# K blocks transposed by DMA instead of by TensorE, in a two-layer decode kernel

## The chip, the cores and the metric

One core of one Trainium2 chip (trn2). The metric is device time of one execution in microseconds (us), on the core. Before the change it is 217.3 us (median of 2 runs, 216.55 to 218.04). A profile's span is 1.7 to 1.9 us shorter than the time of the same run.

## The reference

Decode for a batch of 4, one new token each. Two rounds of attention over a cached window and a gated feed-forward layer (GLU), with the same K, V and weights in both rounds:

```python
x = x + A(layernorm(x), k_cache, v_cache, wq, wo)
x = x + B(layernorm(x), w_gate, w_up, w_down)
x = x + A(...)      # the same caches and weights again
x = x + B(...)

def A(x, k_cache, v_cache, wq, wo):            # B=4, Hq=32, Hkv=8, Dh=128
    W = 2048                                   # last 2048 of 8192 keys
    q = (x @ wq)                               # 4 query heads share one K/V head
    p = softmax(q @ k[:, :, -W:, :].T * Dh**-0.5)
    return (p @ v[:, :, -W:, :]) @ wo
```

There are 32 K blocks and 32 V blocks (8 heads, 4 sequences), each 2048 x 128 bf16, 512 KB.

## The kernel before

The first attention layer loads each K block in a staging slot of SBUF, transposes it on TensorE, and copies it from PSUM to its resident place in `kt`. The second attention layer finds K there and reads V alone again. A list scheduler in the program orders the instructions of each engine; all DMAs are issued by SyncE, in program order.

```python
def kv_d(cache, b, h):          # partition p gets keys 16p..16p+15: rows of 4 KB
    return cache[b, h, SK - W:SK, :].rearrange("(p j) d -> p (j d)", p=128)

def k_head(h):                  # the four K blocks of one head
    for b in range(NB):
        i = h * NB + b
        s = load_block(...)                     # one of 9 staging slots ("arena")
        for t in range(NHALF):                  # 2 halves of 8 columns of 128x128
            # TensorE: 8 transposes into one PSUM bank
            #   pe.transpose(bankb(bank)[:, jj*128:(jj+1)*128], src[:, j*128:(j+1)*128], ident_b)
            # VectorE or ScalarE in turn: copy 128x1024 to kt[:, i*SLOT + ...]
            ...  # cut
        pool.release(s, rel_names)

def e_s(pe, ...):               # scores: K^T is the stationary operand
    for j in range(NJ):         # 16 slices of 128 keys
        pe.matmul(ps[...], kt[:, i*SLOT + j*128 : i*SLOT + (j+1)*128], qT[...])

# program order in the first layer, which is the order of the DMA queue:
#   K(0), wq, then for each head h:  K(h+1), scores(h), V(h), wo(h), PV(h), output(h)
# V, wq and the GLU weights use the same 9 slots.        ... the rest is cut
```

Of the kernel before, what the change touches and what calls it, by code (L numbers as in the profile page):

```python
# [244 lines left out]
class _SlotPool:  # L245
# [29 lines left out]
    bw_4k=338.0, bw_1k=292.0, bw_8k=350.0,  # L275
# [6 lines left out]
def build(nc, A_x, A_k, A_v, A_wq, A_wo, B_wg, B_wu, B_wd, out, cfg=None):  # L282
    cfg = dict(cfg or {})
    tm = dict(_TM)
# [7 lines left out]
    _, HKV, SK, DH = A_k.shape  # L292
    HQ = A_wq.shape[1] // DH
    REP = HQ // HKV
    W = min(4096, max(256, SK // 4))
    NJ = W // 128
# [5 lines left out]
    SLOT = NJ * 128  # L302
# [4 lines left out]
    TB = min(8, NJ)  # L307
    NHALF = NJ // TB
# [20 lines left out]
    def kv_d(cache, b, h):  # L329
        return cache[b, h, SK - W:SK, :].rearrange("(p j) d -> p (j d)", p=128)  # L330

    es = contextlib.ExitStack()
    with es:
        def sb(name, shape, dt):
            return es.enter_context(nc.sbuf_tensor(name, shape, dt))

        kt = sb("kt", [128, NBLK * SLOT], BF16)
        wo_sb = sb("wo_sb", [128, HKV * WOH], BF16)
        arena = sb("arena", [128, NA * SLOT], BF16)
        ident_b = sb("ident_b", [128, 128], BF16)  # L340
# [32 lines left out]
        for _pass in range(cfg.get("passes", 1)):  # L373
            P = _Plan()
            pool = _SlotPool(range(NA), slot_est)

            def slot_ap(s):
                if s < NA:
                    return arena[:, s * SLOT:(s + 1) * SLOT]
                i = s - NA  # L380
                return kt[:, i * SLOT:(i + 1) * SLOT]

            def slot_tok(s):
                if s < NA:
                    return (("slot", s),)
                i = s - NA
                return tuple(("kt", i, t) for t in range(NHALF))
# [4 lines left out]
            def bankb(b):  # L392
                return ps[:, b, :].bitcast(BF16)

            def c_dve(n, rate=None):
                return tm["dve_fix"] + n * (tm["dve_f32"] if rate is None else rate)

            def c_act(n):
                return tm["act_fix"] + n * tm["act_el"]

            def c_pairs(n):
                return n * tm["pe_pair"]

            def dma(name, dst, src, w, r=(), rate="bw_4k", nbytes=None, sem=None):
                if nbytes is None:
                    nbytes = dst.partition_size() * dst.free_nbytes()
                o = P.op("sync", name, 0.0, lambda e, dst=dst, src=src: e.dma_start(dst, src),
                         r=r, w=w, dma_bytes=nbytes, dma_rate=tm[rate])
                if sem is not None:
                    o.sem = sem  # L410
                    o.inc = 16
                return o
# [5 lines left out]
                 r=[("ones_f",)], w=[("ident_f",)])  # L418
            P.op("gpsimd", "ident_b", 200.0, lambda g: g.tensor_copy(ident_b[:], ident_f[:]),
                 r=[("ident_f",)], w=[("ident_b",)])  # L420
# [4 lines left out]
            def emit_xT_in(t):  # L425
                last = None
                for c in range(NC):
# [4 lines left out]
                 w=[("psx", QB)], banks=(QB,))  # L432
            P.op("vector", "xT_cp", c_dve(NX), lambda v: v.tensor_copy(xT[:, :], bankb(QB)[:, 0:NX]),
                 r=[("psx", QB)], w=[("xT",)], banks=(QB,))
# [39 lines left out]
            def load_block(name, cache, b, h):  # L474
                s = pool.alloc()
                dma(name, slot_ap(s), kv_d(cache, b, h), w=slot_tok(s))
                return s

            def attention(L, first, banks):
                TBK = banks["T"]  # L480
# [4 lines left out]
                tcount = [0]  # L485

                def k_head(h):
                    for b in range(NB):
                        i = h * NB + b
                        s = load_block("K%d_%d_%d" % (L, h, b), A_k, b, h)  # L490
                        rel_names = []
                        for t in range(NHALF):
                            bank, ev = TBK[tcount[0] % len(TBK)]
                            tcount[0] += 1

                            def e_tr(pe, s=s, t=t, bank=bank):
                                last = None
                                src = slot_ap(s)
                                for jj in range(TB):
                                    j = t * TB + jj  # L500
                                    last = pe.transpose(bankb(bank)[:, jj * 128:(jj + 1) * 128],  # L501
                                                        src[:, j * 128:(j + 1) * 128], ident_b[:, :])
                                return last
                            P.op("tensor", "T%d_%d_%d" % (L, i, t), TB * tm["pe_tr"], e_tr,
                                 r=list(slot_tok(s)) + [("ident_b",)], w=[("pst", bank)], banks=(bank,))
                            rel_names.append("T%d_%d_%d" % (L, i, t))
                            dst = kt[:, i * SLOT + t * TB * 128: i * SLOT + (t + 1) * TB * 128]
                            if ev == "vector":
                                P.op("vector", "evT%d_%d_%d" % (L, i, t), c_dve(TB * 128, tm["dve_bf_psum"]),
                                     lambda v, dst=dst, bank=bank: v.tensor_copy(dst, bankb(bank)[:, 0:TB * 128]),  # L510
                                     r=[("pst", bank)], w=[("kt", i, t)], banks=(bank,))
                            else:
                                P.op("scalar", "evT%d_%d_%d" % (L, i, t), c_act(TB * 128),
                                     lambda a, dst=dst, bank=bank: a.copy(dst, bankb(bank)[:, 0:TB * 128]),  # L514
                                     r=[("pst", bank)], w=[("kt", i, t)], banks=(bank,))
                        pool.release(s, rel_names)

                if first:
                    k_head(0)
                first_q = True  # L520
                for ktc in range(NC):
                    for qc in range(NQCH):
                        s = pool.alloc()
# [5 lines left out]
                        def e_q(pe, ktc=ktc, q0=q0, q1=q1, s=s, st=first_q):  # L529
                            last = None  # L530
                            src = slot_ap(s)
                            for q in range(q0, q1):
# [8 lines left out]
                             r=list(slot_tok(s)) + [("xn",)], w=[("psq", QB)], banks=(QB,))  # L541
# [4 lines left out]
                     r=[("psq", QB)], w=[("qT",)], banks=(QB,))  # L546

                def scores_softmax(h):
# [5 lines left out]
                    for b in range(NB):  # L554
                        i = h * NB + b

                        def e_s(pe, i=i, b=b, h=h, sbk=sbk):
                            last = None
                            for j in range(NJ):
                                c0 = b * NJ * REP + j * REP  # L560
                                last = pe.matmul(ps[:, sbk, c0:c0 + REP],  # L561
                                                 kt[:, i * SLOT + j * 128: i * SLOT + (j + 1) * 128],
                                                 qT[:, b * HQ + h * REP: b * HQ + (h + 1) * REP],
                                                 start=True, stop=True)
                            return last
                        P.op("tensor", "S%d_%d" % (L, i), c_pairs(NJ), e_s,
                             r=[("kt", i, t) for t in range(NHALF)] + [("qT",)],
                             w=[("pss", sbk, b)], banks=(sbk,))
# [4 lines left out]
                         r=[("pss", sbk, b) for b in range(NB)], w=[("m1", kd)], banks=(sbk,))  # L573
                    P.op("tensor", "smaxT_%d_%d" % (L, h), tm["pe_small"],
                         lambda pe, m1v=m1v, mbk=mbk: pe.transpose(ps[0:NR, mbk, 0:128], m1v, ident_f[:, :]),  # L575
                         r=[("m1", kd), ("ident_f",)], w=[("psm", mbk, 0)], banks=(mbk,))
# [3 lines left out]
                         r=[("psm", mbk, 0)], w=[("gmv", kd)], banks=(mbk,))  # L580
# [3 lines left out]
                         r=[("gmv", kd), ("ones_f",)], w=[("Gb", kd)])  # L584
                    P.op("tensor", "smaxB_%d_%d" % (L, h), tm["pe_small"],
                         lambda pe, Gv=Gv, mbk=mbk: pe.transpose(ps[:, mbk, 128:128 + NR], Gv, ident_f[0:NR, 0:NR]),  # L586
                         r=[("Gb", kd), ("ident_f",)], w=[("psm", mbk, 1)], banks=(mbk,))
# [3 lines left out]
                         r=[("psm", mbk, 1)], w=[("gbc", kd)], banks=(mbk,))  # L591
# [7 lines left out]
                         r=[("pss", sbk, b) for b in range(NB)] + [("gbc", kd)], w=[("d", kd)], banks=(sbk,))  # L599
                    ev = ebuf[:, ke * GC:(ke + 1) * GC]  # L600
                    P.op("scalar", "sexp_%d_%d" % (L, h), c_act(GC),
                         lambda a, ev=ev, dv=dv: a.activation(ev, dv, ACTF.Exp, scale=SCALE),  # L602
                         r=[("d", kd)], w=[("e", ke)])
                    esv = esum[:, kd * NR:(kd + 1) * NR]
                    P.op("vector", "ssum_%d_%d" % (L, h), c_dve(GC),
                         lambda v, ev=ev, esv=esv: v.tensor_reduce(  # L606
                             esv.rearrange("p (b r) -> p b r", b=NB),
                             ev.rearrange("p (b j r) -> p b r j", b=NB, j=NJ, r=REP), AXX, ALU.add),
                         r=[("e", ke)], w=[("es", kd)])
# [3 lines left out]
                         r=[("es", kd), ("ones_f",)], w=[("psm", mbk, 2)], banks=(mbk,))  # L613
# [3 lines left out]
                         r=[("psm", mbk, 2)], w=[("rinv", ke)], banks=(mbk,))  # L617
# [59 lines left out]
            def glu(L, banks):  # L677
# [49 lines left out]
                for (fc0, fc1) in bounds:  # L727
# [24 lines left out]
                T=[(0, "vector"), (2, "scalar"), (1, "vector"), (3, "scalar")], S=[4], M=[6], O=5)))  # L752
# [5 lines left out]
                 r=[("xT",)], w=[("xb16",)])  # L758

            def e_out_tr(pe):  # L760
                last = None
                for c in range(NC):
# [3 lines left out]
                 w=[("pso_f", QB)], banks=(QB,))  # L766
            P.op("vector", "out_cp", c_dve(D, tm["dve_bf_psum"]), lambda v: v.tensor_copy(o_nat[:, :], bankb(QB)[0:NB, 0:D]),
                 r=[("pso_f", QB)], w=[("xnat",)], banks=(QB,))
# [77 lines left out]
```

## Time and profile before

The span splits at the layer norms. This is the timeline of TensorE, at the first matmul of the norm before each layer; columns are start (us), duration (us), engine, line and instruction.

```profile
121.16 0.59 PE L438 MATMUL ps<-lr,ones_f 128*128 128x4 f32 x2 [0.48 <-DVE lr L440]
...
133.00 0.59 PE L438 MATMUL ps<-lr,ones_f 128*128 128x4 f32 x2 [0.48 <-DVE lr L440]
...
202.63 0.59 PE L438 MATMUL ps<-lr,ones_f 128*128 128x4 f32 x2 [0.48 <-DVE lr L440]
```

| stage | ends at | length, us |
|---|---|---|
| first attention layer | 121.16 | 121.2 |
| first GLU | 133.00 | 11.8 |
| second attention layer | 202.63 | 69.6 |
| second GLU, output | 215.5 | 12.9 |

The table of windows has a row for each stretch: its length, then the busy time and instruction count of each engine, the granted TensorE clock, the busy share of the 16 DMA engines (the times of the packets are added up, so it passes 1.0 where they overlap: up to 23 are under way at once in this trace), and GB/s.

```profile
36.00:74.00 38.00, 32.23 (x631) 30.89 (x630) 16.15 (x37) 13.62 (x18) 0.00 (x0) 0.72 1.03 398
74.00:111.00 37.00, 31.23 (x647) 30.03 (x645) 14.62 (x35) 13.62 (x18) 0.00 (x0) 0.68 1.01 373
111.00:121.00 10.00, 4.44 (x114) 3.78 (x111) 2.67 (x10) 0.59 (x2) 0.00 (x0) 0.50 0.79 291
121.00:133.00 12.00, 6.64 (x172) 6.04 (x172) 2.07 (x10) 0.60 (x3) 0.00 (x0) 0.50 0.98 311
144.00:170.00 26.00, 18.65 (x545) 17.70 (x546) 7.95 (x27) 1.77 (x6) 0.00 (x0) 0.50 1.03 408
```

In the first attention layer both sides are nearly full: the DMA engines have a share of 1.0 at about 400 GB/s, and TensorE is busy 85% of the time. The DMA engines are ahead by a hair; from 74 us on the rate sags to 373 GB/s, and from 111 to 121 us there is a hole while TensorE finishes the last head.

The groups of instructions that the change touches (busy time in us, mean ns of one, then the engine's idle time before them), and the K transfers (count, KB each, median us from issue to landing):

```profile
L501 PE MATMUL ps<-ident_b,arena 128*128 128x128 bf16 x512 | 47.5, 279 | 1.1 <-DMA arena<-in_A_k_cache_dram 1.1
...
L514 ACT COPY kt<-ps 128x1024 bf16<-128x1024 bf16 x32 | 31.5, 1015 | 49.9 <-PE ps L501 49.9
L561 PEld LDWEIGHTS ps<-qT,kt 128*128 128x128 bf16 x1024 | 30.6, 102 | 15.9 <-issue 7.8
...
L510 DVE COPY kt<-ps 128x1024 bf16<-128x1024 bf16 x32 | 22.1, 692 | 27.1 <-PE ps L501 27.1
```
```profile
arena<-in_A_k_cache_dram SPq DMA_DIRECT2D x32, 512.0 KB, 8.9
```

So 47.5 us of TensorE work and 53.6 us of copies are to go. The mean of 279 ns is a duration with overlap: 512 x 279 ns would be 143 us. And this is how a burst of score matmuls looks in the timeline: 16 in 0.55 us, about 34 ns each.

```profile
69.52 0.55 PE L561 MATMUL ps<-qT,kt 128*128 128x4 bf16 x16 [0.72 <-DVE dbuf L594]
```

### The profile page before, as it was taken

To read this page: it belongs to the slowest core of one execution; us is meant where nothing else is said; L and a number is where in the kernel's file an instruction comes from. 1 tells how busy PE (TensorE), PEld (TensorE's weight loads), DVE (VectorE), ACT (ScalarE), POOL (GpSimd) and SP (SyncE) were. 2 spreads that over 40 slices of the span, in tenths; PEclk is the share of its full clock that TensorE was granted. 3 is DMA by queue.
4 is the path that set the end of the run, shared out by engine and by line. 5 is a ranking of instruction groups with operands and counts; after the bars stand their busy time and mean duration, and the time that the engine had idled before them with its cause. 6 is when DMAs were issued, how large, how long until landed. Compare 5 with 4: busy or idle time off the path is not lost.

```text
span 215.5 us, 7541 instructions
## 1 busy us (share of the span) xinstructions
PE 152.5 (71%) x3496; PEld 142.9 (66%) x3496; DVE 68.0 (32%) x193; ACT 44.2 (20%) x75; POOL 1.0 (0%) x7
## 2 busy tenths in 40 slices
PE   2944869879696987969673574657758777676664
PEld 2933859779595987959563573546757776566563
DVE  1400353433435343343513211013313422433121
ACT  2610251615325151532501000001101100101000
POOL 1000000000000000000000000000000000000000
PEclk9995595785759585575955555555555555555555
DMA  6999999999999999999997899999999999995000
GB/s 206 332 418 411 408 392 405 395 407 396 400 400 393 401 394 379 309 415 341 368 398 289 270 316 324 420 408 406 407 409 408 408 411 403 403 379 174 3 3 1
DMA packets 26447, 74.42 MB, mean 345 GB/s; under 512 B 2344, under 2 KB 10032, under 8 KB 26416
## 3 DMA queue, kind: packets, MB, share of 16 engines
q1 hardware_dynamic: 26416, 73.94, 90.2%
q8 instruction: 27, 0.44, 0.8%
q14 instruction: 4, 0.03, 0.0%
HBM read 73.93 MB, written 0.00 MB: 343 GB/s over the span
## 4 chain that ended last, share of the span: by engine, by line
PE 60%; DMA 13%; DVE 12%; issue 10%; ACT 3%; SPq 0%; DVEq 0%
PE ps L501 21%; PE ps L636 13%; PE ps L561 10%; DMA arena<-in_A_wq_dram 9%; PE ps L611 3%; PE ps L657 3%; DVE dbuf L594 3%; DVE m L572 3%; DMA arena<-in_B_w_down_dram 2%; PE ps L575 2%; PE ps L586 2%; PE ps L695 2%; DMA arena<-in_A_k_cache_dram 2%; PE ps L737 1%; DVE Gb L583 1%
## 5 line engine op out<-in xcount | busy, mean ns | idle before, releaser
L501 PE MATMUL ps<-ident_b,arena 128*128 128x128 bf16 x512 | 47.5, 279 | 1.1 <-DMA arena<-in_A_k_cache_dram 1.1
L501 PEld LDWEIGHTS ps<-ident_b,arena 128*128 128x128 bf16 x512 | 45.2, 131 | 1.3 <-DMA arena<-in_A_k_cache_dram 1.1
L514 ACT COPY kt<-ps 128x1024 bf16<-128x1024 bf16 x32 | 31.5, 1015 | 49.9 <-PE ps L501 49.9
L561 PEld LDWEIGHTS ps<-qT,kt 128*128 128x128 bf16 x1024 | 30.6, 102 | 15.9 <-issue 7.8
L561 PE MATMUL ps<-qT,kt 128*128 128x4 bf16 x1024 | 32.7, 166 | 11.6 <-DVE dbuf L594 5.1
L510 DVE COPY kt<-ps 128x1024 bf16<-128x1024 bf16 x32 | 22.1, 692 | 27.1 <-PE ps L501 27.1
L636 PEld LDWEIGHTS ps<-ebuf,arena 128*128 128x128 bf16 x800 | 25.9, 106 | 4.9 <-issue 4.4
L636 PE MATMUL ps<-ebuf,arena 128*128 128x4 bf16 x800 | 25.7, 166 | 4.1 <-issue 2.9
L590 ACT COPY gbc<-ps 128x16 f32<-128x16 f32 x16 | 2.8, 172 | 73.0 <-PE ps L586 73.0
L533 PE MATMUL ps<-xn,arena 128*128 128x4 bf16 x256 | 9.3, 166 | 9.9 <-DMA arena<-in_A_wq_dram 7.6
L533 PEld LDWEIGHTS ps<-xn,arena 128*128 128x128 bf16 x256 | 8.0, 102 | 11.3 <-DMA arena<-in_A_wq_dram 8.9
L657 PE MATMUL ps<-onb,wo_sb 128*128 128x4 bf16 x256 | 9.5, 167 | 2.2 <-issue 1.2
L572 DVE TENSOR_REDUCE m<-ps 128x16 f32<-128x256 f32 x16 | 6.7, 422 | 12.7 <-PE ps L561 12.7
L575 PE MATMUL ps<-ident_f,m 128*16 128x128 f32 x16 | 5.3, 334 | 7.4 <-DVE m L572 4.1
L657 PEld LDWEIGHTS ps<-onb,wo_sb 128*128 128x128 bf16 x256 | 8.7, 106 | 2.5 <-issue 1.7
L611 PE MATMUL ps<-esum,ones_f 128*128 128x16 f32 x32 | 8.7, 350 | 2.1 <-DVE esum L606 2.1
L636 PE MATMUL ps<-ebuf,kt 128*128 128x4 bf16 x224 | 7.4, 166 | 3.5 <-issue 3.1
L636 PEld LDWEIGHTS ps<-ebuf,kt 128*128 128x128 bf16 x224 | 7.1, 106 | 4.0 <-issue 3.9
L594 DVE TENSOR_TENSOR dbuf<-ps,gbc 128x256 f32<-128x256 f32 x16 | 6.8, 425 | 9.3 <-ACT gbc L590 9.3
L611 PEld LDWEIGHTS ps<-esum,ones_f 128*128 128x128 f32 x32 | 7.4, 286 | 2.4 <-issue 1.6
L606 DVE TENSOR_REDUCE esum<-ebuf 128x16 f32<-128x256 bf16 x16 | 6.7, 420 | 6.4 <-ACT ebuf L602 6.3
L647 DVE TENSOR_TENSOR onb<-ps,rinv 128x16 bf16<-128x16 f32 x16 | 3.1, 193 | 16.8 <-PE ps L636 16.6
(46 smaller groups left out, 73.9 us busy)
## 6 DMA issues: line engine op xcount, KB each, us to landing
arena<-in_A_v_cache_dram SPq DMA_DIRECT2D x50, 512.0 KB, 9.1
arena<-in_A_k_cache_dram SPq DMA_DIRECT2D x32, 512.0 KB, 8.9
arena<-in_A_wq_dram SPq DMA_DIRECT2D x16, 512.0 KB, 9.6
kt<-in_A_v_cache_dram SPq DMA_DIRECT2D x14, 512.0 KB, 14.1
wo_sb<-in_A_wo_dram SPq DMA_DIRECT2D x8, 512.0 KB, 9.5
arena<-in_B_w_gate_dram SPq DMA_DIRECT2D x5, 448.0 KB, 8.8
arena<-in_B_w_up_dram SPq DMA_DIRECT2D x5, 448.0 KB, 7.1
arena<-in_B_w_down_dram SPq DMA_DIRECT2D x4, 512.0 KB, 5.9
```

The lines of the kernel that those rows point to most:

```text
L501: last = pe.transpose(bankb(bank)[:, jj * 128:(jj + 1) * 128], src[:, j * 128:(j + 1) * 128], ident_b[:, :])
L510: lambda v, dst=dst, bank=bank: v.tensor_copy(dst, bankb(bank)[:, 0:TB * 128]),
L514: lambda a, dst=dst, bank=bank: a.copy(dst, bankb(bank)[:, 0:TB * 128]),
L533: last = pe.matmul(ps[:, QB, q * NB:(q + 1) * NB], src[:, (q - q0) * 128:(q - q0 + 1) * 128], xn[:, ktc * NB:(ktc + 1) * NB], start=(st an ...
L561: last = pe.matmul(ps[:, sbk, c0:c0 + REP], kt[:, i * SLOT + j * 128: i * SLOT + (j + 1) * 128], qT[:, b * HQ + h * REP: b * HQ + (h + 1) ...
L572: lambda v, S4=S4, m1v=m1v: v.tensor_reduce(m1v.rearrange("p (b r) -> p b r", b=NB), S4, AXX, ALU.max),
L575: lambda pe, m1v=m1v, mbk=mbk: pe.transpose(ps[0:NR, mbk, 0:128], m1v, ident_f[:, :]),
L594: lambda v, dv=dv, gbv=gbv, S_all=S_all: v.tensor_tensor(dv.rearrange("p (b j r) -> p b j r", b=NB, j=NJ, r=REP), S_all.rearrange("p (b j ...
L606: lambda v, ev=ev, esv=esv: v.tensor_reduce(esv.rearrange("p (b r) -> p b r", b=NB), ev.rearrange("p (b j r) -> p b r j", b=NB, j=NJ, r=RE ...
L611: lambda pe, esv=esv, mbk=mbk: pe.matmul(ps[:, mbk, 256:256 + NR], ones_f[:, :], esv, start=True, stop=True),
L636: last = pe.matmul(ps[:, OB, b * REP:(b + 1) * REP], src[:, j * 128:(j + 1) * 128], ebuf[:, c0:c0 + REP], start=(j == 0), stop=(j == NJ - 1))
L657: last = pe.matmul(ps[:, OB, 64 + c * NB: 64 + (c + 1) * NB], wo_sb[:, h * WOH + r_ * D + c * 128: h * WOH + r_ * D + (c + 1) * 128], ov[: ...
```

## The change

The intent: K arrives transposed, straight in its resident place, so TensorE, VectorE and ScalarE lose the transposes and their evacuation, and K no longer needs staging slots. The program takes the columns of a transposed block as keys in their natural order, while V's blocks hold keys 16p to 16p+15 in partition p, so the scores now take every 16th column. "Crossbar" below is a name for the path of the DMA_TRANSPOSE instructions.

```diff
                 def k_head(h):
                     for b in range(NB):
                         i = h * NB + b
-                        s = load_block("K%d_%d_%d" % (L, h, b), A_k, b, h)
-                        ...   # 2 x 8 TensorE transposes, 2 evacuations, release of the slot (cut)
+                        P.op("sync", "K%d_%d_%d" % (L, h, b), 0.0,
+                             lambda e, i=i, b=b, h=h: e.dma_start_transpose(
+                                 kt[:, i * SLOT:(i + 1) * SLOT], A_k[b, h, SK - W:SK, :]),
+                             w=[("kt", i, t) for t in range(NHALF)],
+                             dma_bytes=SLOT * 256, dma_rate=tm["bw_4k"])
@@ scores
-                                                 kt[:, i * SLOT + j * 128: i * SLOT + (j + 1) * 128],
+                                                 kt[:, i * SLOT + j: i * SLOT + SLOT: NJ],
```

More of the change, by code (lines that the diff above doesn't have):

```diff
@@ L489, in k_head @@
                         i = h * NB + b
-                        s = load_block("K%d_%d_%d" % (L, h, b), A_k, b, h)
-                        rel_names = []
-                        for t in range(NHALF):
-                            bank, ev = TBK[tcount[0] % len(TBK)]
-                            tcount[0] += 1
-                            def e_tr(pe, s=s, t=t, bank=bank):
-                                last = None
-                                src = slot_ap(s)
-                                for jj in range(TB):
-                                    j = t * TB + jj
-                                    last = pe.transpose(bankb(bank)[:, jj * 128:(jj + 1) * 128],
-                                                        src[:, j * 128:(j + 1) * 128], ident_b[:, :])
-                                return last
-                            P.op("tensor", "T%d_%d_%d" % (L, i, t), TB * tm["pe_tr"], e_tr,
-                                 r=list(slot_tok(s)) + [("ident_b",)], w=[("pst", bank)], banks=(bank,))
-                            rel_names.append("T%d_%d_%d" % (L, i, t))
-                            dst = kt[:, i * SLOT + t * TB * 128: i * SLOT + (t + 1) * TB * 128]
-                            if ev == "vector":
-                                P.op("vector", "evT%d_%d_%d" % (L, i, t), c_dve(TB * 128, tm["dve_bf_psum"]),
-                                     lambda v, dst=dst, bank=bank: v.tensor_copy(dst, bankb(bank)[:, 0:TB * 128]),
-                                     r=[("pst", bank)], w=[("kt", i, t)], banks=(bank,))
-                            else:
-                                P.op("scalar", "evT%d_%d_%d" % (L, i, t), c_act(TB * 128),
-                                     lambda a, dst=dst, bank=bank: a.copy(dst, bankb(bank)[:, 0:TB * 128]),
-                                     r=[("pst", bank)], w=[("kt", i, t)], banks=(bank,))
-                        pool.release(s, rel_names)
+                        P.op("sync", "K%d_%d_%d" % (L, h, b), 0.0,
[3 more added lines that the diff above has]
+                             dma_bytes=SLOT * 256, dma_rate=tm["bw_4k"])
                 if first:
```

## The prediction

> **What bounds the kernel now.** Not TensorE, though PE is busy 71% of the span. In the table of windows, from 10 to 100 us the DMA share is 1.00 to 1.03 at 365 to 411 GB/s, again 1.02 to 1.03 from 132 to 185 us.  74.4 MB at about 405 GB/s is 184 us of a 215.5 us span. In the first attention layer (to about 111 us) K and V (16.8 MB each), wq and wo (4.2 MB each) arrive: 42 MB, about 104 us at that rate. PE (11.1 of 13 us busy in 23-36 us) is close behind. The chain of waits names the transposes (L501, 21% of the span), but the queue's own waits on L501 (32.7 us) never let the DMA engines run dry.
>
> **What the change removes.** 512 transposes (PE 47.5 us), 64 evacuations of 128x1024 (ACT 31.5 us, DVE 22.1 us), and K's use of the nine staging slots. All of it lies in 0-111 us, under saturated DMA. Off the critical path, except: the first K block's transposes before the q projection, the drop to 365-384 GB/s from 74 to 111 us, and the hole at 111-121 us. I give this 3 to 5 us.
>
> **What it adds.** (a) 16.8 MB now cross the transposing path. Today they cost 16.8 MB / 405 GB/s = 41 us of DMA time. [...] Since DMA binds this stage, the difference is exposed nearly whole[...]. [...] (b) The score matmuls now take their stationary operand with a step of 16 elements (32 B): 1024 weight loads, 96 to 104 ns each now at about 26 ns start to start. If the strided read costs 25 ns more, that is 13 us of PE in each attention layer: hidden in the first one, where 47 us of PE work has gone, partly exposed in the second (PE 10.5 of 15 us busy at half clock): +3 to 6 us.
> PE's clock should sit at 0.5 in the first stage instead of 0.62-0.81; there is room for it.
>
> **Sum.** 217.3 - 4 + 19 + 5 = about 238 us; range 213 to 280. Faster by over 2%: 0.13; within 2%: 0.17; slower by over 2%: 0.70.
>
> **What would show each step.** DMA issues: K's time to landing well above 8.9 us. Slices and windows: DMA share still about 1.0 in the first stage, but at 300-350 GB/s where K is under way, with many small packets on the page; a first stage that ends near 125-130 us instead of 111. PE mostly waiting on DMA for kt there; no ACT copies. LDWEIGHTS of the scores longer than 104 ns or score bursts of 64 longer than 1.9 us would show (b). From 132 us on the pace per head of about 7 us should hold or be slightly longer.
>
> **What would make it wrong.** Transposes at 90% or more of copy rate: about 215-220 us. Transposes that serialize with the copies in the same queue, or that are generated slowly by the issuing queue, so that DMA engines idle: 260-300 us. Strided weight loads of 100 ns or more: PE binds the second layer, +25 us.

The sum came to about 238 us. The +19 is the author's guess; the 300-350 GB/s and the 125-130 us among the signs, and the range, rest on it too. The 25 ns in (b), on which the +5 rests, was likewise assumed and not measured.

## The result

255.91 us (median of 2 runs, 255.72 to 256.1) against 217.3: slower, ratio 1.174 (95% interval 1.156 to 1.192). Ratios here are the mean time of one kernel's fast runs over the mean of the other's of the same rounds, so not quite the ratio of the medians quoted.

The layer norms of the kernel after, on TensorE's timeline:

```profile
156.13 0.59 PE L438 MATMUL ps<-lr,ones_f 128*128 128x4 f32 x2 [0.48 <-DVE lr L440]
...
170.48 0.59 PE L438 MATMUL ps<-lr,ones_f 128*128 128x4 f32 x2 [0.48 <-DVE lr L440]
...
241.36 0.59 PE L438 MATMUL ps<-lr,ones_f 128*128 128x4 f32 x2 [0.48 <-DVE lr L440]
```

| stage | before | after | difference |
|---|---|---|---|
| first attention layer | 121.2 | 156.1 | +35.0 |
| first GLU | 11.8 | 14.4 | +2.5 |
| second attention layer | 69.6 | 70.9 | +1.3 |
| second GLU, output | 12.9 | 12.9 | 0.0 |
| span | 215.5 | 254.2 | +38.7 |

The loss is in the one layer in which K arrives. The windows of it, and of the second attention layer:

```profile
36.00:74.00 38.00, 19.32 (x344) 17.07 (x343) 6.29 (x20) 1.45 (x6) 0.00 (x0) 1.00 1.12 281
74.00:111.00 37.00, 18.35 (x325) 16.10 (x322) 5.58 (x18) 1.49 (x5) 0.00 (x0) 1.00 1.13 272
111.00:140.00 29.00, 13.20 (x234) 12.04 (x235) 2.82 (x10) 0.59 (x2) 0.00 (x0) 1.00 1.14 243
...
200.00:220.00 20.00, 20.00 (x403) 19.76 (x403) 6.67 (x22) 1.77 (x6) 0.00 (x0) 1.00 1.03 407
```

TensorE fell from 85% busy to half, as intended. The DMA engines still show a share above 1.0, but move 243 to 281 GB/s instead of about 400: they are occupied, not productive. (The clock of 1.00 is not a reading. The trace of this run has no clock records, and its profile page prints no clock row. Two fp32 matmuls of the layer norm take 0.59 us here, but before they take 0.59 us both at a clock of 1.00, at 2.98 us, and at 0.50, so they tell nothing of it.)

The profile page's count of packets, the score group, the transfers, and what TensorE waits for:

```profile
DMA packets 88393, 74.34 MB, mean 292 GB/s; under 512 B 68392, under 2 KB 76080, under 8 KB 88368
```
```profile
L539 PE MATMUL ps<-qT,kt 128*128 128x4 bf16 x1024 | 70.1, 202 | 35.9 <-DMA kt<-in_A_k_cache_dram 33.4
L539 PEld LDWEIGHTS ps<-qT,kt 128*128 128x128 bf16 x1024 | 67.5, 165 | 38.5 <-DMA kt<-in_A_k_cache_dram 35.4
```
```profile
kt<-in_A_k_cache_dram SPq DMA_TRANSPOSE x32, 5.2
```

K's 16.8 MB come in 65,536 packets of 256 B (before: 4,096 of 4 KB). The landing time of 5.2 us looks better than 8.9, but fewer transfers are ahead of one: when a transfer of K is issued, 2 earlier ones (median) have not landed, where before it was 6. The issue of a transpose itself takes 2.5 us (median; 1.8 at the least), that of a V copy some 0.5 (four in 1.95 us below). First the issues of the transposes (shortest, median and longest in ns), then the shares of the chain of work that ended last:

```profile
L491 SPq DMA_TRANSPOSE kt<-in_A_k_cache_dram x32: 1755/2496/9550, 1.2 to 134.4; - x32
```
```profile
SPq 36%; PE 31%; DMA 26%; DVE 4%; issue 3%; ACT 1%; DVEq 0%
```

SPq is SyncE's issuing of DMAs: 36% of the span lies on it, 31% on the transposes alone, where the chain of the kernel before has 0%. This says where the wait is seen, and not whether the queue or the DMA engines behind it are slow. On the queue's timeline, one head:

```profile
69.61 15.16 SPq L491 DMA_TRANSPOSE kt<-in_A_k_cache_dram  x4
84.87 1.95 SPq L407 DMA_DIRECT2D arena<-in_A_v_cache_dram  x4
86.86 0.66 SPq L407 DMA_DIRECT2D wo_sb<-in_A_wo_dram  x1
```

Four V blocks are issued in 2 us, four transposes in 15. A head takes about 17.7 us from one such line to the next, against 12.6 before (60.84 to 73.46 us there). Short windows of the same stretch show what the engines do in that time:

```profile
75.50:77.00 1.50, 0.98 (x31) 0.81 (x28) 0.30 (x2) 0.00 (x0) 0.00 (x0) 1.00 1.66 141
77.50:78.50 1.00, 0.59 (x16) 0.50 (x16) 0.17 (x1) 0.00 (x0) 0.00 (x0) 1.00 1.28 290
79.00:80.50 1.50, 0.00 (x0) 0.00 (x0) 0.00 (x0) 0.00 (x0) 0.00 (x0) 1.00 1.14 63
81.00:82.00 1.00, 0.99 (x16) 1.00 (x16) 0.00 (x0) 0.00 (x0) 0.00 (x0) 1.00 1.27 286
```

Between them: 290 GB/s is the steady pace inside a transpose (77.5 and 81 us). At 75.5 us the queue goes over from copies to transposes and moves 141 GB/s. At 79 us, inside a run of transposes, it all but stands, with packets in flight.

The single packets in the trace show what stands beside that last stop: a packet of 16 KB on the queue that the profile page calls "instruction" (q8; I take it for a fetch of instructions) starts at 78.68 us and takes 1.08 us. Seven such packets start while transposes are moving (one of them at a change to transposes), and each is followed within 1.5 us by a stop of 1.1 to 1.6 us at 12 to 35 GB/s. Three more in this layer fall among copies, and no such stop follows. Nor does one in the first layer of d_copy4k and c_copy256 below: there the rate stays above 360 and 198 GB/s for 2 us after each such packet. I call these fetch stops. Against the pace of 290 GB/s they cost this kernel about 9.5 us (9.0 to 10.2, by where one sets the rate that counts as a stop; an estimate from the packets). No run varied the fetches, so this is seen in the traces and not shown by an experiment.

And the score bursts are slower with the step of 32 B: 16 in 1.15 us instead of 0.55, so 72 ns for a matmul with its load instead of 34.

```profile
67.35 1.15 PE L539 MATMUL ps<-qT,kt 128*128 128x4 bf16 x16 [0.82 <-DMA kt<-in_A_k_cache_dram]
```

### The profile page after: what moved, and what is told of

Same layout as the page of the kernel before. It is cut to its first block, busy times and chain, and to the rows that moved or that the text cites. A ratio compares the mean times of both kernels' runs of the same rounds, so it can differ in the third digit from the quotient of the medians.

```text
span 254.2 us, 6443 instructions
## 1 busy us (share of the span) xinstructions
PE 150.5 (59%) x2984; PEld 138.1 (54%) x2984; DVE 46.7 (18%) x161; ACT 12.7 (5%) x43; POOL 1.0 (0%) x7
## 4 chain that ended last, share of the span: by engine, by line
SPq 36%; PE 31%; DMA 26%; DVE 4%; issue 3%; ACT 1%; DVEq 0%
SPq L491 31%; PE ps L539 17%; DMA arena<-in_A_wq_dram 8%; DMA kt<-in_A_k_cache_dram 8%; PE ps L614 5%; DMA wo_sb<-in_A_wo_dram 5%; SPq L407 5%; DMA arena<-in_B_w_down_dram 3%; DMA arena<-in_A_v_cache_dram 2%; PE ps L673 1%; PE ps L589 1%; PE ps L715 1%; PE ps L635 1%; PE ps L553 1%; PE ps L438 1%
## 5 line engine op out<-in xcount | busy, mean ns | idle before, releaser
L539 PE MATMUL ps<-qT,kt 128*128 128x4 bf16 x1024 | 70.1, 202 | 35.9 <-DMA kt<-in_A_k_cache_dram 33.4
L539 PEld LDWEIGHTS ps<-qT,kt 128*128 128x128 bf16 x1024 | 67.5, 165 | 38.5 <-DMA kt<-in_A_k_cache_dram 35.4
L614 PEld LDWEIGHTS ps<-ebuf,arena 128*128 128x128 bf16 x800 | 27.5, 108 | 15.4 <-DMA arena<-in_A_v_cache_dram 14.9
L614 PE MATMUL ps<-ebuf,arena 128*128 128x4 bf16 x800 | 28.0, 167 | 12.3 <-DMA arena<-in_A_v_cache_dram 12.2
L589 PEld LDWEIGHTS ps<-esum,ones_f 128*128 128x128 f32 x32 | 8.2, 317 | 6.6 <-ACT ebuf L580 6.6
L553 PE MATMUL ps<-ident_f,m 128*16 128x128 f32 x16 | 6.1, 379 | 4.0 <-DVE m L550 3.6
L438 PE MATMUL ps<-lr,ones_f 128*128 128x4 f32 x16 | 4.7, 365 | 4.7 <-DVE lr L456 2.8
L580 ACT ACTIVATE ebuf<-dbuf 128x256 bf16<-128x256 f32 x16 | 6.7, 417 | 7.8 <-DVE dbuf L572 7.8
L438 PEld LDWEIGHTS ps<-lr,ones_f 128*128 128x128 f32 x16 | 4.0, 311 | 5.4 <-DVE lr L456 3.1
L594 DVE RECIPROCAL rinv<-ps 128x16 f32<-128x16 f32 x16 | 4.1, 258 | 14.5 <-PE ps L589 14.5
## 6 DMA issues: line engine op xcount, KB each, us to landing
arena<-in_B_w_gate_dram SPq DMA_DIRECT2D x5, 448.0 KB, 12.9
arena<-in_B_w_up_dram SPq DMA_DIRECT2D x5, 448.0 KB, 12.9
```

The costliest lines, as they stand in the source:

```text
L438: return t.matmul(dst, ones_f[:, :], src, start=True, stop=True)
L539: last = pe.matmul(ps[:, sbk, c0:c0 + REP], kt[:, i * SLOT + j: i * SLOT + SLOT: NJ], qT[:, b * HQ + h * REP: b * HQ + (h + 1) * REP], sta ...
L553: lambda pe, m1v=m1v, mbk=mbk: pe.transpose(ps[0:NR, mbk, 0:128], m1v, ident_f[:, :]),
L580: lambda a, ev=ev, dv=dv: a.activation(ev, dv, ACTF.Exp, scale=SCALE),
L589: lambda pe, esv=esv, mbk=mbk: pe.matmul(ps[:, mbk, 256:256 + NR], ones_f[:, :], esv, start=True, stop=True),
L614: last = pe.matmul(ps[:, OB, b * REP:(b + 1) * REP], src[:, j * 128:(j + 1) * 128], ebuf[:, c0:c0 + REP], start=(j == 0), stop=(j == NJ - 1))
```

## The experiments

Theory 1: the transposing transfers themselves cost the time, by their packets' pace and by what is lost around them. Rivals: the strided score reads (2), the small packets with no part of the crossbar in it (3), the generation of transposes in the queue (4). The lengths of the layers are read as above. The comparison with the reference doesn't notice a K in the wrong order, and "results right" rests on reading the code too. I take it that the times don't depend on the values; no run tests that.

| run | time, us | ratio to before (95%) | first attention | second attention |
|---|---|---|---|---|
| before | 216.6 to 217.9 | 1 | 121.2 | 69.6 |
| after | 255.91 | 1.174 (1.156 to 1.192) | 156.1 | 70.9 |
| a_contig | 253.5 (fast runs) | 1.165 (1.160 to 1.171) | 158.8 (slow run) | 68.3 (slow run) |
| d_copy4k | 212.10 | 0.975 (0.971 to 0.979) | 112.0 | 70.8 |
| c_copy256 | 248.38 | 1.143 (1.138 to 1.148) | 148.2 | 71.2 |
| e_batched | 247.92 | 1.139 (1.134 to 1.145) | 148.1 | 70.7 |
| f_alternate | 267.36 | 1.227 (1.218 to 1.235) | 167.9 | 70.9 |
| g_halves | 268.31 | 1.232 (1.223 to 1.241) | 167.8 | 70.8 |
| h_actqueue | 301.6 (fast runs) | 1.384 (1.369 to 1.399) | slow run | slow run |
| j_double | 246.46 | 1.133 (1.126 to 1.139) | 146.5 | 70.9 |
| l_batched_double | 240.86 | 1.110 (1.102 to 1.119) | 141.6 | 71.4 |
| b_strided | 233.58 | 1.075 (1.068 to 1.081) | 135.4 | 71.5 |
| i_hybrid | 216.54 | 0.992 (0.985 to 0.999) | 119.4 | 68.3 |
| k_hybrid2 | 213.88 | 0.984 (0.978 to 0.989) | 118.4 | 67.7 |

### a_contig: neighbouring columns for the scores

```diff
-    kt[:, i * SLOT + j: i * SLOT + SLOT: NJ],
+    kt[:, i * SLOT + j * 128: i * SLOT + (j + 1) * 128],
```

> The kernel after with the score matmuls reading 128 neighbouring columns of the transposed block, as before the change (results wrong on purpose). Theory 1 (the crossing transfers themselves cost the time: 290 GB/s in their packets against about 405 for copies, plus lost time at every change between transposes and copies): nothing but the second attention layer moves; 252 to 256 us, the first attention layer still ends near 156 us. Rival 2 (the strided weight loads, 165 ns instead of 96 to 104, slow TensorE, which frees slots late): 220 to 235 us.

Measured 253.5 us (median of the four fast runs; 253.8 with the slow one). Rival 2 is out: with the stride gone the time is only about 2 us lower. (The profiled run was 1.5% above the fastest of this kernel, so its layers are not compared.) That the step makes the bursts slow is shown by its score bursts, back at 0.59 us:

```profile
64.73 0.59 PE L539 MATMUL ps<-qT,kt 128*128 128x4 bf16 x16 [2.73 <-DMA kt<-in_A_k_cache_dram]
```

### d_copy4k: K copied in 4 KB rows, no transpose anywhere

```diff
-    e.dma_start_transpose(kt[:, i*SLOT:(i+1)*SLOT], A_k[b, h, SK - W:SK, :])
+    e.dma_start(kt[:, i*SLOT:(i+1)*SLOT], kv_d(A_k, b, h))
```

> The kernel after with K as plain copies of 4 KB rows into its resident place, no transpose anywhere (results wrong on purpose), strided score reads kept. It prices the removed TensorE work alone. Theory 1: 212 to 217 us, that is the 1 to 5 us which the prediction gave for the removal, with the first attention layer ending at 115 to 121 us. Rival 2 (strided reads bind): above 230 us. If it comes out below 205 us, TensorE bound the kernel before and my reading of the first stage was wrong.

Measured 212.1 us, in the band; the first layer ends at 112.0. This is what the removal is worth when K's transfer costs nothing more:

```profile
36.00:74.00 38.00, 29.05 (x542) 27.24 (x542) 7.97 (x27) 1.76 (x6) 0.00 (x0) 1.00 1.04 401
74.00:100.00 26.00, 17.67 (x316) 15.70 (x314) 5.87 (x19) 1.20 (x5) 0.00 (x0) 1.00 1.03 400
...
111.00:121.00 10.00, 5.51 (x132) 4.86 (x132) 1.97 (x9) 0.60 (x3) 0.00 (x0) 1.00 1.05 385
```

The sag from 74 us on and the hole at 111 us of the kernel before are gone. The layer is 9.1 us shorter (121.2 to 112.0), of which 2.5 are given back in the next one: the first GLU takes 14.3 to 15.2 us instead of 11.8 in the kernels without TensorE transposes (all but h_actqueue, with 11.6 in a slow run). My reading of that is that before, the GLU weights came while TensorE was still behind; I tested it no further. The run takes away the transposes, their evacuations and the staging slots at once, so it doesn't split them. By the same two numbers the transposing transfers cost 156.1 - 112.0 = 44.1 us in the kernel after.

### c_copy256: as many small packets, no crossbar

```diff
+    e.dma_start(kt[:, i*SLOT:(i+1)*SLOT].rearrange("p (j d) -> p j d", d=DH),
+                A_k[b, h, SK - W:SK, :].rearrange("(j p) d -> p j d", p=128))
```

> As the run with 4 KB rows, but K copied in packets of 256 B, as many as the transposes have, without the crossbar (results wrong on purpose). If the small packet alone sets the 290 GB/s (rival 3), K costs 32 x 0.5 = 16 us more than with 4 KB rows: 228 to 234 us, and 20 us below the kernel after, since no time is lost at changes. If small packets cost nothing, it equals the 4 KB run within 2 us and the crossbar is the whole cause. If it comes out at 250 us or more, the crossbar is innocent and 256 B packets explain everything.

Measured 248.4 us, near the third case and in none of the stated bands. A stretch with K alone:

```profile
56.50:65.00 8.50, 2.90 (x48) 2.65 (x48) 0.25 (x2) 0.00 (x0) 0.00 (x0) 1.00 1.18 222
```

Plain copies of 256 B move 222 GB/s, evenly, less than the 290 of a transpose at its best. So packets of 256 B are enough to explain a loss of 36 us (148.2 - 112.0) with no transpose involved. My estimate that they cost 16 us was too small even for copies. This doesn't prove that transposes lose their time in the same way: they run faster than this and then stop.

### e_batched and f_alternate: the same transposes in another order

```diff
 # e_batched: K(1) to K(7) right after the q weights, then all V and wo loads
-    if first and h + 1 < HKV:
-        k_head(h + 1)
+    # before the loop over heads:  for hh in range(1, HKV): k_head(hh)
 # f_alternate: inside pv_wo(h)
+    for b in range(NB):  k_head(h + 1, (b,));  load_block(V(h, b))
```

> The kernel after with the same transposes in another order: after the q weights, the 28 remaining K blocks in one run, then all V and output-weight loads (results right). Changes between transposes and copies fall from 17 to 3. Theory 1 with 1 to 1.3 us lost at each change: 235 to 241 us, and K blocks landing every 1.9 to 2.0 us throughout the run. If changes cost nothing (each transpose simply costs about 2.4 us, wherever it stands; or the issue of a transpose, 1.75 us and more, limits): 250 to 257 us.

Measured 247.9 us, 8 us less, which is in neither band. Changes between transposes and copies seem to cost something, but half of what I expected at most. (Counted out in the order of the queue, the kernel after has 15 changes and not 17, this one 3, the next one 57.) The run of 28 transposes alone:

```profile
46.00:56.00 10.00, 5.48 (x68) 4.87 (x67) 1.66 (x5) 0.59 (x2) 0.00 (x0) 1.00 1.21 196
...
76.00:86.00 10.00, 0.00 (x0) 0.00 (x0) 0.00 (x0) 0.00 (x0) 0.00 (x0) 1.00 1.24 227
```

Even with no copy near, the rate is 196 to 227 GB/s, not 290. (The first window holds a fetch stop, at 50 us. From 76 to 86 us no other engine runs and no instruction packet starts.)

> The kernel after with the loads alternating one K transpose, one V copy (results right): about 60 changes between the two kinds instead of 17. The batched run, with 14 changes fewer, was 8 us faster, 0.55 us a change. Theory 1a (each change costs): 275 to 285 us. Rival 4 (the queue cannot generate a transpose faster than about 2.0 us, and cannot get ahead of copies, so data engines wait for it): with a copy's 1.3 us of data between any two transposes the generation hides, and the time falls to 235 to 250 us.

Measured 267.4 us. Rival 4 is out in the form I gave it: a copy between two transposes hides nothing. The expectation of 275 to 285 was also too high. Here a transpose ends (first line), and then nearly nothing moves for three quarters of a microsecond before the copy runs:

```profile
71.75:72.75 1.00, 0.59 (x16) 0.51 (x16) 0.00 (x0) 0.00 (x0) 0.00 (x0) 1.00 1.28 290
73.00:73.75 0.75, 0.07 (x1) 0.07 (x2) 0.00 (x0) 0.00 (x0) 0.00 (x0) 1.00 0.35 26
74.00:75.00 1.00, 0.83 (x14) 0.74 (x13) 0.00 (x0) 0.00 (x0) 0.00 (x0) 1.00 0.97 331
```

The price of one change, from the lengths of the first layer: (156.1 - 148.1) / 12 = 0.67 us, and (167.9 - 156.1) / 42 = 0.28 us. Part of this difference is in the fetch stops: e_batched has four, worth 5.0 us against 9.5 in the kernel after, and those of f_alternate, which fall on changes for the most part, cost about 6.6. With them taken out the price of a change is 0.29 and 0.35 us (estimates from the packets).

### g_halves and j_double: other sizes of a transpose

```diff
 # g_halves: 64 transposes of 1024 rows
+    for t in range(NHALF): e.dma_start_transpose(kt[half t], A_k[b, h, rows of half t, :])
 # j_double: 16 transposes of 4096 rows (the second block gets other keys: wrong on purpose)
+    for b in range(0, NB, 2):
+        e.dma_start_transpose(kt[:, i*SLOT:(i+2)*SLOT], A_k[b, h, SK - 2*W:SK, :])
```

> The kernel after with every K block as two transposes of 1024 rows (results right), 64 instead of 32. If the dip that stands between two transposes is a cost per instruction (0.2 to 0.4 us), 32 more of them give 262 to 270 us, and the issue of a half still takes well over 1 us. If cost follows the bytes alone, 253 to 258 us and each half's issue takes about 1.0 us.

> The kernel after with 16 transposes of 4096 rows in place of 32 of 2048: each takes the window's rows and the 2048 before them, so that the source is one run (results wrong on purpose; same bytes, same packets). The halves cost 0.39 us for each instruction added. If that is a fixed cost per transpose, 16 fewer save 6 us: 247 to 251 us. If the loss lies with the bytes (256 B packets, stalls inside a run), 254 to 257 us.

Measured 268.3 and 246.5 us, with the same 65,536 packets in all three. So each transpose has a cost of its own beside its bytes: in the first layer 11.6 us for 32 more (0.36 us each), 9.7 us for 16 fewer (0.60 us each). With the fetch stops taken out (7.1 and 6.4 us, against 9.5), the two agree: 0.44 and 0.41 us (estimates). The issues of the halves and of the doubles:

```profile
L493 SPq DMA_TRANSPOSE kt<-in_A_k_cache_dram x64: 1242/1298/5561, 1.2 to 147.8; - x64
```
```profile
L491 SPq DMA_TRANSPOSE kt<-in_A_k_cache_dram x16: 3605/4851/12553, 1.2 to 123.7; - x16
```

By the median an issue takes 1.30, 2.50 and 4.85 us for a half, a whole and a double, so it follows the bytes for the most part; these runs don't show a fixed part of the issue.

### l_batched_double: both savings at once

The edits of e_batched and j_double together (wrong).

> Both at once: all K after the q weights in one run, and 4096 rows in each transpose (results wrong on purpose, as with the 4096-row run). Batching alone saved 8 us, doubling alone 9.4 us. If a cost per transpose (0.59 us x 32 = 19 us) and a cost per change (0.55 us x 15 = 8 us) stand side by side, which with the 16.8 us of the packet rate make up the 44 us that the first layer lost against copies, the savings add up: 237 to 241 us. If both had removed the same loss: 245 to 248 us. Neither reaches the kernel before, as the packet rate of 290 GB/s stays.

Measured 240.9 us, in the band of the first case; the first layer is 141.6 us, 14.6 us shorter than in the kernel after, where the two alone gave 8.0 and 9.7. They add up for the most part, so they are mainly two losses and not one. What is missing from the sum, 3.1 us, is about what the fetch stops give: each edit cut them by itself (4.5 and 3.1 us), and both together by no more than 4.4. And the best order with the largest transposes is still 11% slower than the kernel before.

### h_actqueue: transposes on ScalarE's queue

```diff
-    P.op("sync", "K...", 0.0, ...)
+    o = P.op("scalar", "K...", 2000.0, ..., after=[exponential of head h - 2])
+    o.sem = ("dmaK", i); o.inc = 16          # a semaphore of its own for each block
```

> The kernel after with the 32 transposes issued by ScalarE on its own queue, paced two heads ahead of the exponentials, all copies still on SyncE's (results right[...]). Rival 4 (generation behind copies in one queue costs the time): transposes are made while copies move; 222 to 238 us. Theory 1 (the data engines are slow with these packets): the same bytes pass the same 16 engines, 248 to 260 us.

Measured 299.9 and 303.4 us in the two fast runs (306.6 and 311.4 in the other two), outside both bands. The profile is of a slow run, but all four are far above the bands. ScalarE's timeline shows a reason that has nothing to do with the question:

```profile
65.43 0.42 ACT L584 ACTIVATE ebuf<-dbuf 128x256 bf16<-128x256 f32 x1 [0.49 <-DVE dbuf L576]
65.88 24.26 ACTq L493 DMA_TRANSPOSE kt<-in_A_k_cache_dram  x4
90.18 0.17 ACT L572 COPY gbc<-ps 128x16 f32<-128x16 f32 x1 [24.33 <-issue]
```

ScalarE stands for 24 us issuing four transposes, and the softmax of the next head waits behind them. In this trace the packets of the two queues start in equal numbers: from 55.0 to 55.5 us 48 packets of K (256 B) and 48 of V (4 KB) start, one for one, which is 25 GB/s for K and 393 for V. So K crawls there while copies run. What holds ScalarE in its issue isn't shown. The run does not settle whether generation or the engines limit a transpose.

### b_strided: the strided reads alone, in the kernel before

```diff
-    kt[:, i * SLOT + j * 128: i * SLOT + (j + 1) * 128],
+    kt[:, i * SLOT + j: i * SLOT + SLOT: NJ],
```

> The kernel before with the strided score reads alone, transposes on TensorE and copies kept (results wrong on purpose). In the kernel after a group of 16 such matmuls took 1.15 us against 0.55: about 37 ns more each, 19 us of TensorE time in each attention layer. In the kernel after this cost 2.6 us in all, as TensorE waited anyway. Here TensorE is busy 85 to 90% of the first layer: if it is the second limit there, as I hold, 6 to 12 us come out, plus 1 to 3 in the second attention layer: 225 to 232 us. If the DMA engines alone set the pace: 217 to 221 us.

Measured 233.6 us, just above the band: 14.2 us more in the first layer, 1.8 in the second.

```profile
65.00:79.00 14.00, 12.76 (x207) 12.28 (x206) 4.62 (x11) 3.95 (x5) 0.00 (x0) 0.62 0.84 302
79.00:93.00 14.00, 12.17 (x211) 11.90 (x211) 5.13 (x12) 4.44 (x6) 0.00 (x0) 0.72 0.83 308
```

Now the DMA share is 0.83: TensorE sets the pace. The same 37 ns for each load (1.15 - 0.55 us, over 16) are nearly free in the kernel after and cost 16 us here. It also shows how close TensorE was to being the limit before.

### i_hybrid and k_hybrid2: a few blocks through the crossbar

```diff
 # in the kernel before, k_head:
+    if h >= HKV - 1:                      # k_hybrid2: and b >= NB - 2
+        P.op("sync", ..., e.dma_start_transpose(kt[block i], A_k[b, h, SK - W:SK, :]), ...)
+        continue
 # and strided score reads for those blocks alone
```

> The kernel before with only the last head's four K blocks through the crossbar (results right): candidate for the best of both. Four blocks cost 4 x 0.7 us more transfer and two changes, about 4 us; they take 64 transposes (about 5 us of TensorE) off the end of the first attention layer, where TensorE is last and the DMA engines had a hole (111 to 121 us). Both theories: 214 to 219 us, so within 2% of before; below 213 us would make it worth keeping.

> The hybrid with two of the last head's four blocks through the crossbar instead of four (results right), to see whether less is better: about 2 x 1.0 us less transfer loss, but only half of the 64 transposes gone from the end of the first attention layer. Expected 214.5 to 217.5 us, within 2% of before; a clear gain only below 213 us.

Measured 216.5 and 213.9 us (results right). With two blocks of 32 transposed on the way, which came out a little below its band, the time is 1.65% below the kernel before (0.978 to 0.989, 6 runs against 11): the fastest correct kernel here, though "unclear" and not "faster" by the 2% rule. Its windows beside those of before:

```profile
74.00:111.00 37.00, 31.14 (x655) 29.89 (x654) 14.15 (x35) 11.69 (x16) 0.00 (x0) 0.64 1.03 346
111.00:121.00 10.00, 5.22 (x97) 4.45 (x96) 3.33 (x13) 0.97 (x4) 0.00 (x0) 0.50 1.03 396
121.00:133.00 12.00, 6.60 (x172) 5.93 (x172) 1.79 (x8) 0.22 (x1) 0.00 (x0) 0.50 1.06 383
```

The two transposes cost rate while they run (346 against 373 GB/s), and fill the hole: 396 against 291, then 383 against 311. Of the 3.5 us by which the span is shorter (215.5 to 212.0), the first attention layer and the GLU after it give 1.6. The other 1.9 come in the second attention layer, where the change adds only the strided reads of two blocks; why it is shorter is left open. So the filled hole accounts for less than half of the gain.

## Why the prediction was right, and where it was off

It named the sign, the bound and the place, and 255.9 lies in its range of 213 to 280. That range is 67 us wide, so being inside it says little. Its centre of 238 was 18 us low: the crossing was put 25 us too low, and by luck the removal and the strided reads, each off by about 3 us the other way, made up for some of it.

- "DMA binds this stage, the difference is exposed nearly whole": right. The first attention layer grew by 35.0 of the 38.7 us, with TensorE waiting for K.
- "I give this 3 to 5 us" (the removal): too little. In the first layer it is worth 9.1 us, 5.4 us net in the span with the strided reads in it (215.5 to 210.1). TensorE's work, with its evacuations and slots, was not merely close behind the DMA engines; it held them back from 74 us on. b_strided, which slows TensorE alone, points to TensorE among the three.
- The +19 us of the sum (the crossing): the term that failed, by more than two. It measured +44.1 us against copies of the same bytes. The pace inside a transpose accounts for 16.0 us of it: 290 GB/s is 57.9 us for 16.8 MB, copies at 401 GB/s take 41.9. Plain copies of 256 B moved 222 GB/s, so the size of the packets alone doesn't set the pace, and the reason for the 290 isn't shown. What I left out is that the pace isn't kept. Some 28 us more are lost around it. The runs as they stand give 0.36 to 0.60 us for each of 32 transposes and 0.28 to 0.67 us at each of 15 changes, together 16 to 29 us. With the fetch stops split off, three parts make up the loss: 0.41 to 0.44 us for each transpose (13 to 14 us), 0.29 to 0.35 us at each change (4 to 5 us), and 9.5 us of fetch stops, together 27 to 29 us. All three are estimates from the runs and their packets. The stop at 79 us above is one of the third kind; what in the chip links an instruction fetch to a stop isn't shown.
- "25 ns more", "+3 to 6 us" (the strided reads; the 25 ns was assumed): 37 ns and about 2 us. In the second attention layer TensorE went from 72% to 100% busy and still lost little, as it had slack against the DMA engines.
- How the queue handles a transpose: rival 4, that copies could hide the generation, failed. A fixed cost per transpose stands (0.36 to 0.60 us, above); whether the queue or the engines charge it is open, as is why copies of 256 B run at 222 GB/s.
- Of what would show it: the DMA share stayed at 1.0 or more and TensorE waited for K, as said. The rate was not 300 to 350 but 243 to 281 GB/s, the first layer ended at 156 and not at 125 to 130, and the time to landing fell instead of rising (8.9 to 5.2 us), while the issue rose from some 0.3 us (median of the K copies before) to 2.5. The forecast of PE's clock (0.5; before it was 0.62 to 0.81 from 23 to 111 us, and 0.50 after that) can't be checked, as the trace has no clock records.

## What to carry to other kernels

Here work went from TensorE (85% busy) to the DMA engines, which had a share of 1.0. What it added there was exposed in full (44.1 us in the first layer against plain copies, and 44.1 us in the span: 254.2 against 210.1), and it gained only what TensorE had held back; measure that gain by itself (here with plain copies: 5 us) before paying for it. When you cost a transfer of another kind, count the time it loses around itself, for each instruction, at each change of kind and after instruction fetches (seen here in the traces, not tested), beside its pace, which was here the smaller part of the loss (16 of 44 us). A small dose, placed where the other engine is last and the DMA engines have a hole, may pay where the whole doesn't: 2 blocks of 32 gave 1.65%, of which less than half is explained.
